# Attention tokens regrouped by batch, block 1's inputs held on chip, the inverse RMS passed through memory, constants merged, eight weight units decoded in the attention

## The chip, the cores and the metric

The kernel runs on one core of a Trainium2 chip. The metric is the time of one execution in device microseconds (us); the times of the kernel before are 832.14 us in the median of three runs, from 830.72 to 834.57. The engines are named TensorE (PE in the profile, its weight loads PEld), VectorE (DVE), ScalarE (ACT), GpSimd (POOL) and SyncE (SP). SyncE issues most of the DMAs; ScalarE and GpSimd issue some, each from its own queue of instructions.

## The reference

Four batches of 576 tokens go through a retention layer with 8 heads of 64, a gated MLP with RMS norm, and a mixture of 8 experts, one expert per token:

```python
scores = q @ k.T / sqrt(64)                   # per batch and head
ret = scores * where(rel >= 0, gamma[h] ** rel, 0)
x = (ret @ v).transpose(0, 2, 1, 3).reshape(2304, 512)

rms = sqrt(mean(x * x, -1) + 1e-6)
xn = x / rms * rms_g
g = xn @ w_gate                                # 512 -> 1536
x = (g / (1 + exp(-g)) * (xn @ w_val)) @ w_out # 1536 -> 512

logits = x @ w_gate2 + modality_bias[modality_id]
e = argmax(logits);  gate = softmax(logits)[e]
out = gate * (relu(x @ w1[e]) @ w2[e])         # 512 -> 1024 -> 512
```

The weights of the gated MLP are float32. Every product in the MLP and in the experts is made of three matmuls on high and low parts of both operands.

## The kernel before

The program is one order of instructions per engine, written out by hand; an engine takes its instructions in that order, and a semaphore makes it wait for operands of another engine.

*Attention.* The 576 tokens of a batch are five chunks: four of 128 and one of 64. The 20 steps g (batch b, chunk c) run through a loop over g from 0 to 20. One pass issues: the loads of step g + 7 (`a_load`, two DMAs into one of 8 buffers, SP), the decay of v for step g + 1 (`a_decay`, POOL, L297), the scores of step g (`a_scores`, PE L308, masks on DVE L312), the norm of step g - 3 (`a_norm1`), the running state (`a_state`, PE L327, copies on ACT L332 and L333), the product with V of step g - 1 (`a_pv`, PE L340 and L347, row scaling on DVE L352, square on ACT L354, sums on POOL L361 and L362), for g from 4 to 7 the norm of block 0 (`a_norm2`, DVE, a reciprocal L390 and a multiplication L391), a store of step g - 3 to the DRAM tensor `xnd` (`a_store`, from step 4 on), one tick of the weight pipeline (from pass 11 on) and for g from 7 to 10 the split of block 0's inputs into high and low parts (`split_x`, ACT L216 and DVE L217, four pairs of 128 columns). `a_norm1` sums squares over the partitions with a matmul against ones (L374) and takes the square root on ACT; from step 4 on the steps are summed in groups of up to 512 tokens, and a group's root goes to the DRAM tensor `rmsd` in one row.

*Weight units.* Each weight comes as 64-bit pieces that are rebuilt to 128x512 float32 on chip. A unit has three parts: `s0` the load (SP, 512 KB), `s1` the decode (ACT L135, DVE L136, L139, L142) and `s2` the split into high and low part (ACT L146, DVE L147). `pipe` issues per tick: `s1` of unit i, `s2` of unit i - 2, `s0` of unit i + lead. There are 24 units for the gate and value weights (two per feature tile f) and 12 for the output weights. Four of the first kind and one of the second go through the attention's passes (`prep_a`, lead 4, ticks from pass 11, the remaining ones behind the loop), the others through block 0 of the MLP (`prep_b`, lead 2; the last unit is cut in two halves).

*MLP.* The 2304 tokens are six blocks of 512, 512, 384, 384, 256 and 256. A block runs over 12 feature tiles f: `gv_mm` for gate and value (24 matmuls with as many columns as the block has tokens, PE L224 to L226), `gv_post` (SiLU on ACT L776, product on DVE L777, cast on ACT L778, difference on DVE L779), and the output product of tile f - 1 (`out_acc`, 3 matmuls of 512 columns per 128 tokens). In block 0 each f also carries 3 ticks of `prep_b`, f = 0, 4 and 8 carry 4. At f = 3 the inputs of the next block are loaded (`load_x`, and a row of `rmsd` sent to all partitions), from f = 5 on four pieces of `norm_x` (two reciprocals L199, two multiplications L202) prepare them, and behind f = 11 they are split. The routing of a finished block (per 128 tokens eight dot products L798, two groups of small operations on DVE, a matmul and an indirect store) is spread over the feature tiles of the next block as `bg`, `rate` pieces per f. The dot products write their unused full result into a part of the tile of the next block's inputs.

*Between attention and MLP.* The first gate product (`g0`), then `a_norm1` of the last two steps, then the first value product (`v0`).

*Experts.* Nine visits with fixed capacities read the tokens back by expert, with weights loaded and split on the way, and scatter the rows to the output by token number.

## Time and profile before

| | us |
|---|---|
| median of three runs | 832.14 |
| the runs, lowest and highest | 830.72, 834.57 |
| the profiled execution, whole time | 832.61 |
| its span from first to last instruction | 830.8 |

The page of the profile gives these busy times and slices:

```profile
PE 796.8 (96%) x4974; PEld 687.9 (83%) x4974; DVE 514.9 (62%) x1187; ACT 288.2 (35%) x555; POOL 98.2 (12%) x148
...
PE   8979889888999999999999999999999999999995
...
DVE  3878688887455636674563675747574555566650
...
PEclk9999999999999999999999999999999999999998
DMA  9997854337810000100100100051735264777400
```

Each of the 40 digits is a slice of 20.8 us, in tenths busy. The attention fills the first four and a half, block 0 the next five, the other blocks go on to slice 27 and the experts fill the rest. A timeline lists instructions by start and duration in us with engine, line and operation; the number in brackets is how long the engine was idle before and what released it. Matmul ends are modelled, so starts are the better measure there.

### The profile page before, as it was taken

How to read it: one execution, taken by the hardware profiler on the slowest of the kernel's cores; microseconds unless marked ns; L12 is line 12 of the kernel's file. 1: busy time of each engine (PE TensorE's matmuls, PEld its weight loads, DVE VectorE, ACT ScalarE, POOL GpSimd, SP SyncE). 2: the span in 40 equal slices, each digit the busy share in tenths (PEclk: the TensorE clock that was granted, in tenths of full speed). 3: DMA queues.
4: the chain of work that ended last, by engine and by line, in shares of the span. 5: the costliest groups of instructions: out<-in, count | busy, mean ns of one | idle time of the engine just before them, and what ended most of it. 6: DMA issues, size and time to landing. Idle time of an engine off the chain costs nothing.

```text
span 830.8 us, 13136 instructions
## 1 busy us (share of the span) xinstructions
PE 796.8 (96%) x4974; PEld 687.9 (83%) x4974; DVE 514.9 (62%) x1187; ACT 288.2 (35%) x555; POOL 98.2 (12%) x148
## 2 busy tenths in 40 slices
PE   8979889888999999999999999999999999999995
PEld 6868667656888889999999999999888898889894
DVE  3878688887455636674563675747574555566650
ACT  5445544434211131113111312134453444455530
POOL 4556100000000000100000001000100010010100
PEclk9999999999999999999999999999999999999998
DMA  9997854337810000100100100051735264777400
GB/s 313 323 360 225 267 202 152 98 117 270 287 61 14 13 14 25 51 14 14 33 13 14 45 15 27 14 189 68 253 123 174 77 217 145 277 249 235 142 19 13
DMA packets 48264, 107.21 MB, mean 129 GB/s; under 512 B 11266, under 2 KB 20998, under 8 KB 48072
## 3 DMA queue, kind: packets, MB, share of 16 engines
q1 hardware_dynamic: 43974, 96.37, 34.8%
q0 software_dynamic: 3168, 9.59, 3.0%
q8 instruction: 40, 0.66, 0.3%
q10 hardware_dynamic: 1058, 0.40, 0.2%
q14 instruction: 24, 0.20, 0.1%
HBM read 84.43 MB, written 22.83 MB: 129 GB/s over the span
## 4 chain that ended last, share of the span: by engine, by line
PE 76%; DVE 14%; issue 4%; ACT 2%; DMA 2%; POOL 1%; SPq 0%; another core or an unknown queue 0%; DVEq 0%; POOLq 0%; ACTq 0%
PE gv L224 10%; PE gv L225 10%; PE gv L226 10%; PE acc L224 10%; PE acc L226 10%; PE acc L225 10%; PE h L224 5%; PE h L225 4%; PE h L226 4%; DVE rawbt L139 2%; DVE rawbt L142 2%; DVE w L147 2%; DVE rawbt L136 1%; DVE pt L312 1%; PE tp L754 1%
## 5 line engine op out<-in xcount | busy, mean ns | idle before, releaser
L224 PE MATMUL gv<-xh,w 128*128 128x512 f32 (+2 forms) x576 | 196.5, 341 | 0.4 <-ACT scratch L776 0.4
L225 PE MATMUL gv<-xo,w 128*128 128x512 f32 (+2 forms) x576 | 194.1, 337 | 0.0
L226 PE MATMUL gv<-xh,w 128*128 128x512 f32 (+2 forms) x576 | 194.1, 337 | 0.0
L224 PEld LDWEIGHTS gv<-xh,w 128*128 128x128 f32 x576 | 109.2, 190 | 10.5 <-ACT scratch L776 0.9
L225 PEld LDWEIGHTS gv<-xo,w 128*128 128x128 f32 x576 | 109.2, 190 | 9.6 <-issue 0.4
L226 PEld LDWEIGHTS gv<-xh,w 128*128 128x128 f32 x576 | 109.1, 189 | 8.2 <-DVE w L147 0.3
L777 DVE TENSOR_TENSOR scratch<-gv,scratch 128x512 f32<-128x512 f32 (+2 forms) x72 | 39.9, 554 | 113.2 <-PE gv L226 113.1
L778 ACT CAST hh<-scratch 128x512 fp32r<-128x512 f32 (+2 forms) x72 | 37.0, 514 | 186.6 <-DVE scratch L777 186.6
L224 PE MATMUL acc<-wo,hh 128*128 128x512 f32 x216 | 86.9, 402 | 8.8 <-ACT hh L778 8.8
L707 DVE TENSOR_TENSOR w<-raw,w 128x1024 fp32r<-128x1024 f32 x64 | 78.1, 1225 | 27.0 <-ACT w L706 26.4
L798 DVE CUSTOM_DVE_ANT_0 xl<-row,wr 128x512 bf16<-128x512 f32 x128 | 87.8, 686 | 5.1 <-DMA xl<-xnd 2.5
L225 PE MATMUL acc<-wo,hh 128*128 128x512 f32 x216 | 86.3, 400 | 4.3 <-DVE wo L147 4.3
L224 PE MATMUL h<-xt,w 128*128 128x256 f32 (+3 forms) x288 | 88.9, 309 | 0.0
L226 PE MATMUL h<-xt,w 128*128 128x256 f32 (+3 forms) x288 | 87.4, 303 | 0.0
L225 PE MATMUL h<-xt,w 128*128 128x256 f32 (+3 forms) x288 | 87.3, 303 | 0.0
L226 PE MATMUL acc<-wo,hl 128*128 128x512 f32 x216 | 86.6, 401 | 0.0
L776 ACT ACTIVATE scratch<-gv 128x512 f32<-128x512 f32 (+2 forms) x72 | 35.3, 490 | 145.1 <-PE gv L226 131.6
L706 ACT CAST w<-raw 128x1024 fp32r<-128x1024 f32 x64 | 65.9, 1041 | 2.2 <-DMA raw<-in_w_dram 2.2
L779 DVE TENSOR_TENSOR hl<-scratch,hh 128x512 fp32r<-128x512 f32 (+2 forms) x72 | 40.2, 559 | 41.8 <-ACT hh L778 41.8
L224 PE MATMUL acc<-w,rh 128*128 128x512 f32 (+1 forms) x160 | 63.7, 398 | 0.0
L225 PE MATMUL acc<-w,rh 128*128 128x512 f32 (+1 forms) x160 | 63.3, 396 | 0.0
L226 PE MATMUL acc<-w,rl 128*128 128x512 f32 (+1 forms) x160 | 63.3, 395 | 0.0
(217 smaller groups left out, 1163.8 us busy)
## 6 DMA issues: line engine op xcount, KB each, us to landing
raw<-in_w_dram SPq DMA_DIRECT2D x64, 512.0 KB, 4.7
rawb<-in_wgv_dram SPq DMA_DIRECT2D x20, 512.0 KB, 3.5
xs<-zero SPq DMA_DIRECT2D x8, 1056.0 KB, 12.8
qk<-in_qkt_dram SPq DMA_DIRECT2D x16, 512.0 KB, 7.6
vk<-in_vkn_dram SPq DMA_DIRECT2D x16, 512.0 KB, 8.7
rawb<-in_wout_dram SPq DMA_DIRECT2D x10, 512.0 KB, 3.8
rowc<-xs SPq DMA_DIRECT2D x19, 264.0 KB, 4.4
xnd<-x SPq DMA_DIRECT2D x11, 256.0 KB, 6.2
```

The source lines that it names most:

```text
L139: DVE.scalar_tensor_tensor(out=u, in0=hw, scalar=-0x40000000, in1=u, op0=ALU.bitwise_and, op1=ALU.bitwise_or)
L142: DVE.tensor_tensor(out=u, in0=u, in1=lw, op=ALU.add)
L224: PE.matmul(ps, lh, rh, start=start, stop=False)
L225: PE.matmul(ps, lh, rl, start=False, stop=False)
L226: PE.matmul(ps, ll, rh, start=False, stop=stop)
L706: ACT.copy(out=w[:, 0, :], in_=raw)
L707: DVE.tensor_tensor(out=w[:, 1, :], in0=raw, in1=w[:, 0, :].bitcast(F32), op=ALU.subtract)
L776: ACT.activation(out=h, in_=gps[:, :n], func=ACTF.Silu)
L777: DVE.tensor_tensor(out=h, in0=vps[:, :n], in1=h, op=ALU.mult)
L778: ACT.copy(out=hh[:, :n], in_=h)
L779: DVE.tensor_tensor(out=hl[:, :n], in0=h, in1=hh[:, :n].bitcast(F32), op=ALU.subtract)
L798: DVE.tensor_tensor_reduce(out=junk, in0=row[:, 0:DM].rearrange("p (a b) -> p a b", a=2), in1=wr[:, e, :].rearrange("p (a b) -> p a b", a= ...
```

## The change

Six things, in the order of the file:

1. The blocks are 512, 512, 512, 256, 256, 256 tokens, and the tokens have another order: first the four whole chunks of batch 0, of batch 1, 2 and 3, then the four half chunks, two to a group of 128 (`home`). Three blocks are so the whole chunks of one batch. The token numbers in the rows, the modality and the bias follow that order.
2. Block 0's outputs of the attention stay in one tile `x0`, block 1's in the tile that takes the MLP's inputs (`x1`), and neither is stored; the others go to `xnd` in rows of 128 x 512, contiguous, half chunks in pairs.
3. `a_norm1` acts once per group (a batch's whole chunks, and the four half chunks) and puts the tokens on the partitions: one matmul with one column per 128 tokens, a root and a reciprocal of 128 x 4. The inverse goes to the DRAM tensor `rinv` from ACT's queue in the next pass (`a_inv`), and is read back by `load_inv` to all partitions, for block 0 in pass 9, also from ACT's queue. `norm_x` is then two multiplications of 128 x 1024 per 512 tokens, without reciprocal.
4. Block 0's norm and split are six pieces taken one per pass from pass 11 on (`bg0`): two multiplications and four splits, each of 512 columns.
5. Constants come in four DMAs instead of twelve: `early` (356 KB, ahead of the second step's loads), `keep` in pass 3, `brief` in pass 9, and `lcst` late. The second half of the loads of a 64-token step (k, which is not used there) is left out. The dot products of the routing write to a tile of their own, `sink`.
6. Eight gate and value units and one output unit go through the attention, with ticks from pass 4 on and 5 load buffers instead of 6; `prep_b` keeps 28 units.

The diff, cut to its core:

```diff
-BLOCKS = [512, 512, 384, 384, 256, 256]
+BLOCKS = [512, 512, 512, 256, 256, 256]
...
-XB = 7
+XB = 5
...
-NL2 = 4
-SX = 7
-NUA = 4
-PA, LD, RB = 11, 4, 6
+LX0, NX0 = 9, 11
+NUA = 8
+PA, LD, RB = 4, 4, 5
...
-    xnd = dram.tile([KD, 128, NT], F32, name="xnd")
-    rmsd = dram.tile([1, NT], F32, name="rmsd")
+    xnd = dram.tile([NC, 128, KD * 128], F32, name="xnd")
+    rinv = dram.tile([NT // 512 + 1, 512], F32, name="rinv")
...
+    def load_inv(j, rl, q=SP):
+        gr, o = divmod(STARTS[j], 512)
+        w = min(512, NT - gr * 512)
+        q.dma_start(out=rl[:, :w], in_=rinv[gr:gr + 1, :w].to_broadcast([128, w]))
+        return rl[:, :w].rearrange("p (t c) -> p c t", t=128)[:, o // 128:(o + BLOCKS[j]) // 128]
...
     def norm_x(j, xl, rl):
...
-        return [lambda: inverse(0), lambda: inverse(n // 2), lambda: scale(0), lambda: scale(2)]
+        def scale(c):
+            x, r = xl[:, c:c + 2], rl[:, c:c + 2]
+            DVE.tensor_tensor(out=x, in0=x, in1=r.unsqueeze(2).to_broadcast([128, 2, KD, 128]), op=ALU.mult)
+
+        return [lambda c=c: scale(c) for c in range(0, BLOCKS[j] // 128, 2)]
...
-    def split_x(x, parts, o, n):
+    def split_x(x, parts, n):
+        def piece(k):
+            hi, lo = (z[:, :n].rearrange("p (c t) -> p c t", t=128) for z in parts[k])
+            src = x[:, :n // 128, k, :]
+            ACT.activation(out=hi, in_=src, func=ACTF.Copy, scale=gt[:, k:k + 1])
...
+        return [lambda k=k: piece(k) for k in range(KD)]
...
+        groups = [[g for g in range(G) if steps[g][0] == b and steps[g][3] == 128] for b in range(B)]
+        groups.append([g for g in range(G) if steps[g][3] < 128])
...
+        def home(g):
+            b, c, o, n = steps[g]
+            return (b * NS0 + c, 0) if n == 128 else (B * NS0 + b * n // 128, b * n % 128)
...
+            w = DM if c + 1 == len(CHUNKS) else 2 * DM
+            SP.dma_start(out=vk.rearrange("p a d -> p (a d)")[:n, :w], in_=vkn[b, o:o + n, :w])
...
         def a_norm1(g):
...
+            for i in range(m):
+                PE.matmul(ss[:, i:i + 1], sq[:, i * 128:i * 128 + 128], ones, start=True, stop=True)
+            ri = att.tile([128, NS0], F32, tag="ri", name="ri", bufs=2)
+            ACT.activation(out=ri[:, :m], in_=ss[:, :m], func=ACTF.Sqrt, scale=1.0 / DM, bias=eps[:, 0:1])
+            DVE.reciprocal(out=ri[:, :m], in_=ri[:, :m])
+            i = home(gr[0])[0] // NS0
+            inv.append((rinv[i:i + 1, :n].rearrange("o (t c) -> (o t) c", c=m), ri[:, :m]))
+
+        def a_inv():
+            for dst, src in inv:
+                ACT.dma_start(out=dst, in_=src)
+            inv.clear()
...
             if g < G:
                 a_scores(g)
+            a_inv()
             if g >= 3:
                 a_norm1(g - 3)
+            if g == LX0:
+                bg0 += norm_x(0, x0, load_inv(0, rl0, ACT)) + split_x(x0, xsp, 512)
             if g < G:
                 a_state(g)
             if g >= 1:
                 a_pv(g - 1)
-            if NL2 <= g < NL2 + NS0:
-                a_norm2(g - NL2)
-            if g >= SD + NS0:
+            if g >= NX0 and bg0:
+                bg0.pop(0)()
+            if g >= SD:
                 a_store(g - SD)
...
-            if 0 <= g - SX < NS0:
-                split_x(x_t.pop(g - SX), xsp, 128 * (g - SX), 128)
...
         g0 = gv_mm(0, 0, xsp, BLOCKS[0])
         a_norm1(G - 2)
         a_norm1(G - 1)
+        a_inv()
         v0 = gv_mm(0, 1, xsp, BLOCKS[0])
...
-                    junk = x_in[0].bitcast(BF16)[:, 0:2, 768:1024]
+                    junk = sink.rearrange("p (a b) -> p a b", a=2)
...
-                    x_in[:] = [load_x(j + 1)]
-                    norm = norm_x(j + 1, x_in[0], row_tile(F32, "rl") if j else wr[:, 0, :])
+                    x_in[:] = [load_x(j + 1) if j else x1]
+                    rl = row_tile(F32, "rl") if j else wr[:, 0, :]
+                    norm = norm_x(j + 1, x_in[0], load_inv(j + 1, rl))
```

## Rows read from the trace of the kernel before

**Rows 1.** ScalarE's timeline at the first SiLU or ReLU of a block: start, duration, line, operation

```profile
212.52 0.60 ACT L776 ACTIVATE scratch<-gv 128x512 f32<-128x512 f32 x1 [2.11 <-PE gv L226]
...
311.73 0.49 ACT L776 ACTIVATE scratch<-gv 128x384 f32<-128x384 f32 x1 [1.47 <-PE gv L226]
...
462.77 0.38 ACT L776 ACTIVATE scratch<-gv 128x256 f32<-128x256 f32 x1 [0.80 <-PE gv L226]
...
566.93 0.38 ACT L899 ACTIVATE rh<-h 128x256 fp32r<-128x256 f32 x1 [1.49 <-PE h L226]
```

**Rows 2.** stage of block 4: us, busy PE, PEld, DVE, ACT, POOL; clock, DMA share, GB/s

```profile
461.00:512.00 51.00, 51.00 (x365) 47.30 (x364) 34.12 (x110) 11.40 (x29) 4.20 (x9) 1.00 0.09 30
```

**Rows 3.** VectorE's timeline in block 0: start, duration, line, operation, count

```profile
96.97 0.69 DVE L777 TENSOR_TENSOR scratch<-gv,scratch 128x512 f32<-128x512 f32 x1 [5.00 <-PE gv L226]
...
107.79 0.68 DVE L777 TENSOR_TENSOR scratch<-gv,scratch 128x512 f32<-128x512 f32 x1
...
117.25 0.68 DVE L777 TENSOR_TENSOR scratch<-gv,scratch 128x512 f32<-128x512 f32 x1
...
157.60 1.75 DVE L199 RECIPROCAL wr<-wr 128x256 f32<-128x256 f32 x1
...
179.74 1.22 DVE L202 TENSOR_TENSOR xl<-xl,wr 128x1024 f32<-128x1024 f32 x1
...
180.87 0.69 DVE L777 TENSOR_TENSOR scratch<-gv,scratch 128x512 f32<-128x512 f32 x1
```

**Rows 4.** TensorE's timeline, in brackets idle time before and what ended it

```profile
21.15 0.49 PE L374 MATMUL ss<-sq,ones 128*128 128x128 f32 x2
...
34.08 1.16 PE L308 MATMUL sc<-qk 64*128 64x128 f32 x16
...
91.46 1.73 PE L374 MATMUL ss<-sqs,ones 128*128 128x448 f32 x2 [2.29 <-POOL sqs L362]
...
195.35 0.50 PE L224 MATMUL acc<-wo,hh 128*128 128x512 f32 x1 [1.99 <-ACT hh L778]
```

**Rows 5.** busy us by stage, batches 1 to 3, and a stretch behind them

```profile
23.50:41.60 18.10, 17.65 (x264) 15.16 (x262) 17.28 (x25) 7.34 (x19) 10.60 (x13) 1.00 0.99 312
41.60:65.20 23.60, 18.97 (x262) 15.32 (x261) 16.14 (x30) 11.06 (x28) 12.38 (x19) 1.00 1.08 343
65.20:86.10 20.90, 19.29 (x284) 16.35 (x282) 19.21 (x36) 9.71 (x20) 12.55 (x15) 1.00 0.75 234
...
91.40:95.00 3.60, 3.54 (x7) 2.34 (x8) 0.57 (x1) 1.23 (x2) 0.01 (x1) 0.53 0.73 208
```

**Rows 6.** VectorE's timeline in loops 7 and 8 of the attention

```profile
35.09 0.93 DVE L390 RECIPROCAL ri<-ri 128x128 f32<-128x128 f32 x1
36.06 1.20 DVE L391 TENSOR_TENSOR x<-x,ri 128x512 f32<-128x512 f32 x1
...
39.23 1.27 DVE L312 TENSOR_TENSOR pt<-sc,causal 128x512 f32<-128x512 f32 x2
...
42.47 2.47 DVE L217 SCALAR_TENSOR_TENSOR xo<-x,gt,xh 128x128 fp32r<-128x128 f32 x4 [1.38 <-ACT xh L216]
```

**Rows 7.** VectorE's timeline in loop 17 of the attention

```profile
74.99 1.27 DVE L312 TENSOR_TENSOR pt<-sc,causal 128x512 f32<-128x512 f32 x2
...
76.79 0.41 DVE L136 TENSOR_SCALAR rawt<-raw 128x512 int32<-128x512 int32 x1
...
78.22 0.85 DVE L142 CUSTOM_DVE_ANT_0 rawt<-raw,rawt 128x1024 uint16<-128x1024 uint16 x1 [0.30 <-ACT raw L135]
78.99 0.94 DVE L147 TENSOR_TENSOR w<-rawt,w 128x512 fp32r<-128x512 f32 x1
79.86 1.28 DVE L312 TENSOR_TENSOR pt<-sc,causal 128x512 f32<-128x512 f32 x2
```

**Rows 8.** DMA issues, the rms gains' load: count, KB, us to landing

```profile
gt<-in_rmsg_dram SPq DMA_DIRECT2D x1, 2.0 KB, 8.5
```

**Rows 9.** one line's operations, L147: min/median/max ns, first and last start

```profile
L147 DVE TENSOR_TENSOR w<-rawbt,w x20: 683/684/687, 104.7 to 197.2; 128x512 fp32r<-128x512 f32 x20
```

More of the change, by code (lines that the diff above doesn't have):

```diff
@@ L265 @@
         G = len(steps)
-        qk_t, vk_t, pt_t, x_t, sq_t, ri_t = {}, {}, {}, {}, {}, {}
-        groups, sums = [], {}
-        for g in range(NS0, G):
-            n = steps[g][3]
-            if not groups or sum(steps[i][3] for i in groups[-1]) + n > 512:
-                groups.append([])
-            groups[-1].append(g)
-        place = {g: (gr, sum(steps[i][3] for i in gr[:z])) for gr in groups for z, g in enumerate(gr)}
+        qk_t, vk_t, pt_t, x_t, sums, bg0, inv = {}, {}, {}, {}, {}, [], []
+        groups = [[g for g in range(G) if steps[g][0] == b and steps[g][3] == 128] for b in range(B)]
+        groups.append([g for g in range(G) if steps[g][3] < 128])
+        place = {g: (gr, sum(steps[i][3] for i in gr[:z])) for gr in groups for z, g in enumerate(gr)}
+        x0 = att.tile([128, NS0, KD, 128], F32, name="x0")
+        rl0 = att.tile([128, 512], F32, name="rl0")
+        x1 = x_tile()
+        def home(g):
+            b, c, o, n = steps[g]
+            return (b * NS0 + c, 0) if n == 128 else (B * NS0 + b * n // 128, b * n % 128)
         def by_pair(ps):
@@ L350, in a_pv @@
                     )
-            x = att.tile([128, NP, 128], F32, tag="x", name="x", bufs=XB)
-            DVE.tensor_tensor(out=x[:, :, :n], in0=pv[:, :, :n], in1=rc[:, :, o:o + n], op=ALU.mult)
-            sq = att.tile([128, NP, 128], F32, tag="sq", name="sq", bufs=4)
-            ACT.activation(out=sq[:, :, :n], in_=x[:, :, :n], func=ACTF.Square)
-            total = sq[:, 0, :n]
-            if g >= NS0:
-                gr, o = place[g]
-                if not o:
+            hc, ho = home(g)
@@ new lines, in a_pv @@
+            if hc < 2 * NS0:
+                x = (x0 if hc < NS0 else x1)[:, hc % NS0]
+            else:
+                if not ho:
+                    x_t[hc] = att.tile([128, NP, 128], F32, tag="x", name="x", bufs=XB)
+                x = x_t[hc][:, :, ho:ho + n]
+            DVE.tensor_tensor(out=x, in0=pv[:, :, :n], in1=rc[:, c, :, :n], op=ALU.mult)
+            sq = att.tile([128, NP, 128], F32, tag="sq", name="sq", bufs=4)
+            ACT.activation(out=sq[:, :, :n], in_=x, func=ACTF.Square)
@@ L359, in a_pv @@
+            gr, o = place[g]
+            if not o:
+                if n == 128:
                     sums[gr[0]] = att.tile([128, 512], F32, tag="sqs", name="sqs", bufs=2)
-                total = sums[gr[0]][:, o:o + n]
+                else:
+                    sums[gr[0]] = att.tile([128, 256], F32, name="sqh")
             POOL.tensor_tensor(out=sq[:, 0:2, :n], in0=sq[:, 0:2, :n], in1=sq[:, 2:4, :n], op=ALU.add)
-            POOL.tensor_tensor(out=total, in0=sq[:, 0, :n], in1=sq[:, 1, :n], op=ALU.add)
@@ L363, in a_pv @@
-            x_t[g], sq_t[g] = x, sq
+            POOL.tensor_tensor(out=sums[gr[0]][:, o:o + n], in0=sq[:, 0, :n], in1=sq[:, 1, :n], op=ALU.add)
         def a_norm1(g):
-            n, sq = steps[g][3], sq_t.pop(g)[:, 0, :]
-            if g >= NS0:
-                gr, o = place[g]
-                if g != gr[-1]:
-                    return
-                n, sq = o + n, sums.pop(gr[0])
-            ss = ps_g("ss")
-            PE.matmul(ss[:, :n], ones, sq[:, :n], start=True, stop=True)
-            if g < NS0:
-                ri = att.tile([128, 128], F32, tag="ri", name="ri", bufs=3)
-            else:
-                ri = att.tile([128, 512], F32, tag="rig", name="rig", bufs=2)
@@ L379, in a_norm1 @@
[L379 to L393 removed]
+            gr, o = place[g]
@@ new lines, in a_norm1 @@
+            if g != gr[-1]:
+                return
+            n, sq = o + steps[g][3], sums.pop(gr[0])
+            m = n // 128
+            ss = ps_g("ss")
+            for i in range(m):
[3 more added lines that the diff above has]
+            DVE.reciprocal(out=ri[:, :m], in_=ri[:, :m])
@@ L423 @@
             a_load(g)
-        SP.dma_start(out=ident, in_=cst[:, 0:128])
         POOL.memset(ones16, 1.0)
@@ L465 @@
                 POOL.memset(cum, 0.0)
-            if g == 11:
-                SP.dma_start(out=m64, in_=mod.bitcast(I32).rearrange("p (c two) -> p c two", two=2))
-                SP.dma_start(out=b8, in_=bias)
+            if g == 9:
+                SP.dma_start(out=temp, in_=brief)
             if g == 14:
@@ L767 @@
         wr = bp.tile([128, E, DM], F32, name="wr")
+        sink = bp.tile([128, DM], BF16, name="sink")
         def scratch():
```

152 lines of the change are left out of this document (61 added, 91 removed).

## Prediction

> **What bounds the kernel now.** I read the busy time by stage first, then the timelines of VectorE, TensorE and ScalarE at the seams between stages. Call loop g the g-th of the 20 attention steps, unit one 128x512 weight tile to be rebuilt from its 64-bit form, tick one call of the pipeline that does it, and f the 12 feature tiles of a block of the first MLP.
>
> From block 1 to the end of block 5 TensorE has no idle time: between the first SiLU of block 1 and the first ReLU of the expert stage lie 354.4 us [rows 1], and in block 4 it is busy 51.00 of 51.00 us [rows 2]. VectorE's savings there are worth nothing. The losses sit earlier. In block 0 the MULT of VectorE (L777) comes every 9.46 us (107.79 to 117.25) [rows 3] where block 1 shows that TensorE can do a feature tile in 8.27 us (99.2 us for twelve from 212.52 to 311.73) [rows 1]: VectorE has 1.98 us of its own there (two products and the wait for the cast between them) and three ticks of 2.49 us (9.46 - 1.98 over 3). Feature tiles 0, 4 and 8 carry four ticks, two carry a reciprocal of 1.66 us and two a scaling of 1.13 us [rows 3]. TensorE's last idle time in it ends at 195.35, behind L777 of f = 9 [rows 3, 4]. In the attention both engines are nearly full in batch 1 (TensorE 17.65, VectorE 17.28 of 18.10 us), batch 2 takes 23.60 us for the same work of TensorE and batch 3 20.90 us [rows 5]. So block 0 pays 98.38 us from its first L777 (96.97) to that last stall, and what the change moves is VectorE's work, from block 0 into the attention.
>
> **Attention, loops 0 to 8.** Removed: in loops 4 to 7 a reciprocal (0.97 us start to start) and a scaling (about 1.15 us), in loops 7 to 10 four split products (2.1 to 2.5 us, with up to 1.38 us of waiting for ScalarE ahead) [rows 6]. Without them VectorE has nothing but the masks and the row scaling, 1.8 us per loop, until ticks compute. The masks of loop 8 started at 39.23 although the scores were there from 34.08 + 1.1 = 35.2 [rows 4, 6]. They follow the scores now, so 35.2, and three sums over partitions of some 0.4 us each (0.49 as recorded [rows 4]) leave TensorE's path ahead of that while one group's eight short ones enter (0.3 us, an estimate by their count): 34.3 us, 4.9 us earlier. The merged constant load of 356 KB stands where 28, 64 and 256 KB stood; what the first decay waits for is longer, but the first scores stand behind the warm-up and the second decay behind its own load. Costed at nothing, from -0.5 to +0.5 us.
>
> **Attention, loops 8 to 16.** Nine units instead of five now decode inside the loop, the decode at loops 8 to 16, the split at 10 to 18. A full loop with both cost 4.87 us (74.99 to 79.86), 0.87 of it the last product and 0.3 a wait for ScalarE [rows 7]. Loop 8 has no split: 4.0. Loop 9, with 64 tokens in place of 128: 3.5. Loop 10: 4.6. Loops 11 and 12 add block 0's scaling of 128x1024, 1.13 us as in [rows 3]: 6.0 each. Loops 13 to 16 add one split of 128x512 each: the wait for ScalarE's square and cast (about 1.2 us, as the 1.38 us ahead of the product at 42.47 [rows 6]) and the product (0.65 us, an estimate by the 0.6 to 0.7 us of every 128x512 product here), less the 0.3 us wait that then lies within: 6.4, loop 14 with half the masks and the bias arithmetic 6.9, loop 15 5.9, loop 16 6.4. Sum 49.7 us. Then loops 17 to 19 and the last product with V: before 11.1 us (74.99 to 86.10), now without the two decodes of 2.2 us in it [rows 5, 7]: 6.7. The attention ends at 34.3 + 49.7 + 6.7 = 90.7, 4.6 us later than 86.10.
>
> **Its tail.** From 86.10, the end of batch 3 [rows 5], to the first L777 [rows 3] lie 10.87 us. [...] With no tick left in loop 19 the sums come while the first gate product runs. 10.87 - 3.9 = 7.0, so the first L777 stands at 97.7, 0.7 later than before. The two stores of the inverse and their wait for VectorE's reciprocal stand ahead of the SiLU on ScalarE; one such store and its issue stood there before. Bounds for this 5.5 to 9 us.
>
> **Block 0.** To L777 of f = 8 VectorE took 83.9 us (96.97 to 180.87) [rows 3]. The ticks per feature tile are the same in number; gone are two reciprocals (3.3), and both of block 1's scalings instead of one now come before that point (+1.1): 81.7. There the two kernels part: of 28 units only two half ones and the last splits are left, some 6.3 us with VectorE's own 1.98, so f = 8 no longer binds and TensorE runs at 8.27 from then on. Its resumption at f = 9, 98.38 us after the first L777 before, comes at 81.7 + 1.4 + 8.3 = 91.4: 7.0 us gained. Weights are two tiles further ahead, so the small waits for output weights go too; they are inside the 9.46.
>
> **The rest.** 512, 384, 384, 256, 256 columns become 512, 512, 256, 256, 256. By the seams of [rows 1] a 512 block takes 99.2 us, a 384 block 75.5 (462.77 - 311.73, halved), a 256 one 52.1 (566.93 - 462.77, halved): 151.3 against 151.0 us, +0.3. Block 3 (256) now routes the four chunks of a 512 block; block 4 before routed three with VectorE busy 34.12 of 51 us [rows 2], and one chunk more is eight dot products and two groups of small operations, an estimate of 34.12/3 less the products of the block itself, some 8 us: 42 of 52. It fits; 0 to 2 us if its lag outgrows the PSUM buffers. Reciprocals, the separate sink of the dot products and contiguous loads are off the path. The same tokens go to the same experts, so the expert stage is unchanged.
>
> **DMA.** The weights of eight units (4.2 MB) now go ahead of the last attention load, about 1.8 MB of stores and half vk loads go away. The queue is full until batch 2 ends (share 0.99 to 1.08) but 0.75 in batch 3 [rows 5], so it was ahead of the engines by then, and the attention takes 4.6 us longer. I take nothing; up to 5 us if the queue falls behind in loops 10 to 13. The inverse is written as 128 pieces of 16 bytes at loop 7 and read at loop 9, two loops (about 8 us) later. Nearest is the load of 16-byte pieces, 8.5 us to landing in the full queue [rows 8]: ScalarE, which issues the read, could wait 0 to 2 us, with the copies of the state queued behind it and TensorE's products behind those; I take 0, since ScalarE has no full loop there.
>
> **The sum.** +0.7 - 7.0 + 0.3 = -6.0 us on the profiled execution (832.61, of which its span is 830.8 and 1.8 lie around it, taken as unchanged): 826.6. The median, 832.14, is 0.5 lower: 826.
>
> **Rivals.**
> 1. *VectorE and POOL collide more.* The last product of a unit takes 0.94 us at 78.99 in the attention, where POOL works beside it, and 0.684 (median) in block 0, where POOL is idle [rows 7, 9]. My loops hold that as measured. If the other two-input products are lengthened by the same 0.26 us, it is 18 more of the nine units, four splits and two scalings: 24 x 0.26 = 6, so 832. For it: the scaling of 128x512 at 36.06 took 1.20 us, the one of 128x1024 in block 0 1.22 [rows 3, 6]. Against: in the loops at 74.99 the same POOL work runs and the sum fits. [...]
> 2. *Loads fall behind.* As above, +5: 831. Decides when a load lands after its decay could start.
> [...]
> 4. *The attention is no longer than before.* If the waits for ScalarE vanish in the longer loops and the catch-up at the end is better than 6.7, the 4.6 us do not arise: 821.
> 5. *The change does not move the work.* If block 0 stays bound elsewhere, the 7.0 go: 833.
>
> **How the numbers follow.** Forecast 0.50 (own range 822 to 830), rival 1 0.13, 2 0.10, 3 0.09, 4 0.14, 5 0.04. The likeliest gives 826. From 820 to 834 leaves out half of rival 4 and rival 3. About 0.5% is what a measurement of this kernel can tell from no change: under 828.0 is faster, over 836.3 slower. Over four fifths of the forecast and all of rival 4 are faster: 0.57. Most of rival 3 is slower: 0.08. The rest 0.35.
>
> **What would show it.** Masks of loop 8 near 34; loops 11 to 16 near 6 us with VectorE without idle time; the last product with V near 91; no idle time of TensorE ahead of the sums; first L777 near 98; feature tile 8 at 8.3 us; block 0 about 7 us shorter from the first L777; blocks 1 to 5 again 354 us. Clock under 1 in the attention, a decay that waits for vk, or idle TensorE in block 3 would make it wrong, and so would an attention of other length than 91 us.

## The result, and the profile after

The changed kernel takes 842.16 us (median of 4 runs, 841.26 to 843.00) against 832.71 us (4 runs, 830.72 to 834.57) for the kernel before, both measured side by side: a ratio of 1.0114, 95% interval 1.0085 to 1.0142. It is 1.1% slower; the forecast was 826, with a range of 820 to 834. The profiled execution has a span of 841.2 us, 10.4 more than before, and a mean granted clock of 0.974 (before 0.993).

Where the time came from is read at the seams first. ScalarE's and VectorE's timelines of the kernel after, at the first MULT of block 0 (L782, the L777 of before), the first SiLU of block 1 and the first ReLU of the experts:

```profile
112.77 0.69 DVE L782 TENSOR_TENSOR scratch<-gv,scratch 128x512 f32<-128x512 f32 x1 [2.57 <-PE gv L229]
...
223.59 0.60 ACT L781 ACTIVATE scratch<-gv 128x512 f32<-128x512 f32 x1 [2.16 <-PE gv L229]
...
577.78 0.38 ACT L906 ACTIVATE rh<-h 128x256 fp32r<-128x256 f32 x1 [1.49 <-PE h L229]
```

Against [rows 1] the first SiLU of block 1 is 11.1 us late (223.59 against 212.52), the first ReLU 10.9 us (577.78 against 566.93). So blocks 1 to 5 take 354.2 us as before, and everything was lost ahead of block 1. The first MULT of block 0 came at 112.77 against 96.97 [rows 3], 15.8 us late; from there to block 1 the change won 4.7. The attention lost it. Three stretches of it (us, busy PE, PEld, DVE, ACT, POOL, then clock, DMA share, GB/s):

```profile
39.90:67.60 27.70, 20.20 (x268) 17.14 (x266) 24.86 (x34) 10.11 (x22) 14.85 (x15) 0.92 1.04 358
67.60:86.00 18.40, 15.86 (x136) 13.93 (x136) 14.77 (x25) 7.58 (x16) 7.68 (x10) 0.50 0.16 63
86.00:104.00 18.00, 14.39 (x159) 11.81 (x158) 13.72 (x23) 6.14 (x13) 6.76 (x8) 0.87 0.23 78
```

VectorE is busy 24.86 of 27.70 us in the first, which holds loops 9 to 12 and most of their ticks, TensorE only 20.20; and TensorE's clock, 1.00 in batches 1 to 3 before [rows 5], stands at 0.92, 0.50 and 0.87. Two causes offer themselves, and both are in these rows: a VectorE with no time left, and a TensorE at half its clock. VectorE's timeline at the masks of loop 8, its row scaling, and the masks of loops 14, 15 and 17:

```profile
34.53 1.29 DVE L322 TENSOR_TENSOR pt<-sc,soon 128x512 f32<-128x512 f32 x2 [0.39 <-PE sc L318]
37.28 0.69 DVE L368 TENSOR_TENSOR xl<-pv,soon 128x512 f32<-128x512 f32 x1 [1.45 <-PE pv L357]
...
72.43 0.74 DVE L322 TENSOR_TENSOR pt<-sc,soon 64x256 f32<-64x256 f32 x2
...
80.37 1.28 DVE L322 TENSOR_TENSOR pt<-sc,soon 128x512 f32<-128x512 f32 x2
...
94.69 1.28 DVE L322 TENSOR_TENSOR pt<-sc,soon 128x512 f32<-128x512 f32 x2
```

VectorE's timeline of loop 12, from its masks to those of loop 13, with GpSimd's of the same time:

```profile
57.31 1.27 DVE L322 TENSOR_TENSOR pt<-sc,soon 128x512 f32<-128x512 f32 x2
58.51 0.67 DVE L368 TENSOR_TENSOR x<-pv,soon 128x512 f32<-128x512 f32 x1
59.10 2.06 DVE L205 TENSOR_TENSOR x<-x,rl 128x1024 f32<-128x1024 f32 x1
61.08 0.42 DVE L132 TENSOR_SCALAR rawt<-raw 128x512 int32<-128x512 int32 x1
61.54 1.10 DVE L135 SCALAR_TENSOR_TENSOR rawt<-raw,rawt 128x512 int32<-128x512 int32 x1
62.78 0.72 DVE L138 CUSTOM_DVE_ANT_0 rawt<-raw,rawt 128x1024 uint16<-128x1024 uint16 x1
63.42 1.53 DVE L143 TENSOR_TENSOR w<-rawt,w 128x512 fp32r<-128x512 f32 x1
64.87 1.27 DVE L322 TENSOR_TENSOR pt<-sc,soon 128x512 f32<-128x512 f32 x2
...
60.01 2.09 POOL L377 TENSOR_TENSOR sq<-sq 128x256 f32<-128x256 f32 x1 [3.17 <-ACT sq L370]
62.17 0.78 POOL L378 TENSOR_TENSOR sqs<-sq 128x128 f32<-128x128 f32 x1
62.91 1.48 POOL L307 TENSOR_TENSOR vk<-vk,soon 64x512 f32<-64x512 f32 x1
```

There is no idle time in these 7.56 us, where the forecast had 6.0. The scaling (L205) takes 2.06 us where [rows 3] has 1.22; the second decode step (L135) takes 1.10 and the last product of a unit (L143) 1.53, where a product of this size takes 0.68 with GpSimd idle [rows 9]. The last two began while a GpSimd operation ran (L377 and L307); the scaling began ahead of one (59.10 against 60.01). GpSimd's operations too are long: the decay (L307) takes 1.48 here, and 1.04 in an earlier loop, where VectorE has next to no work:

```profile
27.96 1.04 POOL L307 TENSOR_TENSOR vk<-vk,soon 128x512 f32<-128x512 f32 x1
```

The groups of VectorE's operations of loops 10 to 19 (count, busy us, mean ns, idle time before them), and what it waited for in the same stretch (total, times, longest):

```profile
L135 DVE SCALAR_TENSOR_TENSOR rawt<-raw,rawt 128x512 int32<-128x512 int32 x7 | 8.5, 1220 | 0.2
L143 DVE TENSOR_TENSOR w<-rawt,w 128x512 fp32r<-128x512 f32 x8 | 7.3, 912 | 1.3 <-ACT w L142 1.3
L132 DVE TENSOR_SCALAR rawt<-raw 128x512 int32<-128x512 int32 x7 | 4.8, 683 | 1.2 <-DMA raw<-in_wgv_dram 1.2
L205 DVE TENSOR_TENSOR x<-x,rl 128x1024 f32<-128x1024 f32 x2 | 4.1, 2054 | 0.0
...
DVE xo L219 <- ACT xh L218: 5.3, 4, 1.4
DVE w L143 <- ACT w L142: 1.3, 1, 1.3
DVE wo L143 <- ACT wo L142: 1.3, 1, 1.3
```

### The profile page after: what moved, and what is told of

Same layout as the page of the kernel before. It is cut to its first block, busy times and chain, and to the rows that moved or that the text cites. A ratio compares the mean times of both kernels' runs of the same rounds, so it can differ in the third digit from the quotient of the medians.

```text
span 841.2 us, 13114 instructions
## 1 busy us (share of the span) xinstructions
PE 808.1 (96%) x4994; PEld 689.5 (82%) x4994; DVE 505.7 (60%) x1161; ACT 283.3 (34%) x540; POOL 105.0 (12%) x148
## 4 chain that ended last, share of the span: by engine, by line
PE 77%; DVE 12%; DMA 4%; issue 4%; ACT 2%; POOL 1%; SPq 0%; another core or an unknown queue 0%; DVEq 0%; POOLq 0%; ACTq 0%
PE gv L227 10%; PE gv L229 10%; PE gv L228 10%; PE acc L227 10%; PE acc L229 10%; PE acc L228 10%; PE h L227 4%; PE h L228 4%; PE h L229 4%; DVE rawbt L135 2%; DMA vk<-in_vkn_dram 2%; DVE w L143 2%; DVE rawbt L138 1%; DMA raw<-in_wgv_dram 1%; PE tp L758 1%
## 5 line engine op out<-in xcount | busy, mean ns | idle before, releaser
L227 PE MATMUL gv<-xh,w 128*128 128x512 f32 (+1 forms) x576 | 196.1, 340 | 0.2 <-ACT scratch L781 0.2
L229 PE MATMUL gv<-xh,w 128*128 128x512 f32 (+1 forms) x576 | 194.5, 338 | 0.0
L228 PE MATMUL gv<-xo,w 128*128 128x512 f32 (+1 forms) x576 | 194.4, 338 | 0.0
L782 DVE TENSOR_TENSOR scratch<-gv,scratch 128x512 f32<-128x512 f32 (+1 forms) x72 | 40.0, 556 | 124.9 <-PE gv L229 124.8
L783 ACT CAST hh<-scratch 128x512 fp32r<-128x512 f32 (+1 forms) x72 | 37.0, 514 | 192.5 <-DVE scratch L782 192.5
L803 DVE CUSTOM_DVE_ANT_0 sink<-row,wr 128x512 bf16<-128x512 f32 x128 | 88.2, 689 | 2.6
L781 ACT ACTIVATE scratch<-gv 128x512 f32<-128x512 f32 (+1 forms) x72 | 35.3, 491 | 138.6 <-PE gv L229 132.7
L784 DVE TENSOR_TENSOR hl<-scratch,hh 128x512 fp32r<-128x512 f32 (+1 forms) x72 | 40.2, 559 | 41.8 <-ACT hh L783 41.8
```

The lines of the kernel that those rows point to most:

```text
L227: PE.matmul(ps, lh, rh, start=start, stop=False)
L228: PE.matmul(ps, lh, rl, start=False, stop=False)
L229: PE.matmul(ps, ll, rh, start=False, stop=stop)
L781: ACT.activation(out=h, in_=gps[:, :n], func=ACTF.Silu)
L782: DVE.tensor_tensor(out=h, in0=vps[:, :n], in1=h, op=ALU.mult)
L783: ACT.copy(out=hh[:, :n], in_=h)
```

## Theories and experiments

*Theory A*: VectorE's chain in loops 10 to 16 sets the length; the four more units, the dear scaling, the waits and the stretched operations stand in it. *Theory B* (rival 3, a clock that falls in the attention): TensorE's halved clock sets the length. *Theory C*: on GpSimd the decay of the next chunk is queued behind the square sums, which wait for a late VectorE; the state products wait for the decay. Every run below is compared with the kernel before on the same chip, where that took 832.3 to 832.7 us. "End" is the start of the last row scaling on VectorE, "f = 0" the first MULT of block 0, "block 1" its first SiLU; all in us, from the profiled run.

| kernel | time | ratio, 95% interval | end | f = 0 | block 1 |
|---|---|---|---|---|---|
| before | 832.71 | | 89.06 | 96.97 | 212.52 |
| after | 842.16 | 1.0114 (1.0085-1.0142) | 103.97 | 112.77 | 223.59 |
| a_nua4 | 830.65 | 0.9975 (0.9964-0.9986) | 90.78 | 98.03 | 211.98 |
| b_nua8b | 836.65 | 1.0063 (1.0046-1.0080) | 96.97 | 105.19 | 215.89 |
| a_fill | 844.30 | 1.0150 (1.0133-1.0167) | 106.85 | 114.00 | 224.49 |
| a_dec | 842.91 | 1.0131 (1.0114-1.0148) | 103.35 | 111.92 | 222.75 |
| a_ct | 845.18 | 1.0165 (1.0143-1.0187) | 107.73 | 114.99 | 223.96 |
| a_swap | 836.87 | 1.0063 (1.0046-1.0080) | 99.68 | 106.84 | 217.29 |
| a_swcp | 833.83 | 1.0023 (1.0011-1.0035) | 97.62 | 104.83 | 213.80 |
| a_pesum | 854.12 | 1.0257 (1.0224-1.0290) | 115.54 | 123.78 | 233.86 |
| a_best1 | 824.38 | 0.9913 (0.9896-0.9929) | 86.57 | 92.53 | 204.91 |
| a_best2 | 842.08 | 1.0126 (1.0109-1.0143) | 102.47 | 110.26 | 222.56 |
| a_best3 | 825.10 | 0.9927 (0.9910-0.9943) | 87.36 | 92.67 | 205.57 |
| a_best4 | 828.79 | 0.9969 (0.9954-0.9984) | 92.55 | 97.85 | 208.94 |

**Which part of the change it is: a_nua4 and b_nua8b.** One undoes the units alone (their number, first pass and load buffers), the other makes them alone. b_nua8, the second without its last edit, needs 147.25 KB per partition for the attention's tiles where 145.625 KB are left, and has no time.

```diff
 # a_nua4, on the kernel after
-NUA = 8
-PA, LD, RB = 4, 4, 5
+NUA = 4
+PA, LD, RB = 11, 4, 6
 # b_nua8b, on the kernel before; the second "rig" tile goes to make room
-NUA = 4
-PA, LD, RB = 11, 4, 6
+NUA = 8
+PA, LD, RB = 4, 4, 5
-    ri = att.tile([128, 512], F32, tag="rig", name="rig", bufs=2)
+    ri = att.tile([128, 512], F32, tag="rig", name="rig", bufs=1)
```

> The changed kernel with the weight units of the attention put back to four, from loop 11 on, with six raw buffers; all other parts of the change stay. Theory A (VectorE's work in loops 10 to 16, made by the four extra units) expects the last product of the attention at 87 to 91 us instead of 103.9, the first gv product of block 0 (f = 0) at 95 to 98 instead of 112.8, block 0 longer again by some 4 to 6 us, and a span of 828 to 832. Theory B (the halved TensorE clock) expects the same end only if the clock of loops 11 to 19 is back at 0.95 or more. A rival, that not the units but the six pieces of block 0's norm and split in loops 11 to 16 make the loss, expects the attention to end after 96 and a span of 836 or more.

> The kernel before with one part of the change alone: eight weight units in the attention from loop 4 on and five raw buffers; to find room for them one of the two tiles for the root of a group's mean goes. Theory A (the four extra units lengthen VectorE's chain in the attention by more than block 0 gives back) expects the last product of the attention 7 to 14 us later than 86.1, block 0 some 3 us shorter, and a time of 836 to 844 us. The rival, that the units cost this much only beside the six pieces of block 0 that the change puts into loops 11 to 16, expects the attention to end before 91 and a time of 828 to 834.

With four units the end is back at 90.78 and f = 0 at 98.03, as theory A had it. This alone does not part theory A from theory B, as the clock is back too (1.00 from 39.9 to 67.6 us, 0.91 from there to 86). The four units cost 13.2 us of attention (103.97 - 90.78) and give back 3.1 in block 0, less than the 4 to 6 expected: from f = 0 to block 1 it takes 110.8 us with eight (223.59 - 112.77), 113.95 with four (211.98 - 98.03). The rest of the change together is worth -0.25% (830.65 against 832.47 on that chip): a small gain. On the kernel before, the same units cost 8.2 us up to f = 0 and give back 4.9: 836.65, within the bounds, though at their low end. Up to 1.2 of the 8.2 us may be the missing tile's and not the units', since ScalarE's first SiLU waits there for the store of the root to land, which it does not in the kernel before (1.23 us before it starts at 104.56). So the units lose by themselves, by some 3 to 4 us, and by 11.5 us in the surroundings that the other parts of the change make. One difference shows in VectorE's groups from loop 8 on (count, busy us, mean ns) of b_nua8b:

```profile
L139 DVE SCALAR_TENSOR_TENSOR rawt<-raw,rawt 128x512 int32<-128x512 int32 x9 | 6.2, 693 | 0.3
L136 DVE TENSOR_SCALAR rawt<-raw 128x512 int32<-128x512 int32 x9 | 3.7, 412 | 0.0
```

The same nine units (eight and one output weight), and their first two decode steps take 0.69 and 0.41 us, not 1.22 and 0.68 as L135 and L132 after the change.

**Is it the clock? a_fill.**

```diff
+        def filler(g, ps):
+            if g >= 10:
+                for _ in range(6):
+                    PE.matmul(ps, ones16, wide, start=True, stop=True)   # wide: 128 x 512, BF16
         # a_scores(g), ahead of its products
+            filler(g, scs[0].rearrange("p a t -> p (a t)"))
         # a_pv(g - 1), ahead of its products
+            filler(g + 1, pv.rearrange("p a t -> p (a t)"))
```

> The changed kernel with filler products on TensorE in loops 10 to 19: six of 128 x 512 in BF16 ahead of the scores and six ahead of the value products, into the same PSUM tiles, whose results are overwritten. VectorE's work is untouched. Theory B (the clock sets the length) expects a granted clock of 0.95 or more between 67 and 104 us, score and value bursts near 1.1 us instead of 2.1, the attention's end at 98 or before (103.9 without filler) and a span of 835 or less. Theory A (VectorE's chain sets the length, the clock is only its consequence) expects the clock to rise as well, the attention's end within 1.5 us of 103.9, and a gain of 1 to 2 us at most, from the first gv product, which ran at a clock of 0.57: a span of 839 to 842.

The stretches of the kernel with the filler (columns as above), and the masks of loops 14 and 15:

```profile
39.90:67.60 27.70, 27.19 (x292) 18.55 (x297) 23.76 (x34) 9.45 (x20) 14.59 (x14) 1.00 1.00 348
67.60:86.00 18.40, 17.43 (x175) 11.73 (x177) 14.07 (x26) 7.76 (x16) 7.36 (x10) 1.00 0.26 95
86.00:104.00 18.00, 17.02 (x180) 11.93 (x180) 13.73 (x22) 6.67 (x14) 6.78 (x9) 1.00 0.15 48
...
73.94 0.74 DVE L329 TENSOR_TENSOR pt<-sc,soon 64x256 f32<-64x256 f32 x2
...
81.88 1.28 DVE L329 TENSOR_TENSOR pt<-sc,soon 128x512 f32<-128x512 f32 x2
```

The clock is at 1.00 in all three, and loop 14 takes 7.94 us (73.94 to 81.88), the same as after the change at a clock of 0.50 (72.43 to 80.37); so does loop 15 with 6.86 us in both (81.88 to 88.74, and 80.37 to 87.23). Theory B falls for the loops: with TensorE's waits filled the clock stays up, and the low clock had cost nothing there. What it did cost is behind them: from the end to f = 0 the changed kernel takes 8.80 us, this one 7.15, so 1.65 us is the price of the low clock in the first gate product (0.57 from 104 to 108 us after the change). The end itself comes 2.9 us later than after the change, where theory A allowed 1.5: loop 10 takes 7.62 us instead of 6.13, and VectorE waits 1.54 us for the last product with V. Hence 844.3.

**Is it GpSimd's queue? a_dec.**

```diff
-            if g + 1 < G:
-                a_decay(g + 1)
+            if g == 0:
+                a_decay(1)
+            if g + 2 < G:
+                a_decay(g + 2)
```

> The changed kernel with the GpSimd decay of a chunk issued one loop earlier (two chunks ahead), so that it no longer stands behind the square sums of the loop before. Theory C (the decay queued behind the sums delays the state products, and with them the clock) expects the state product's waits of 3.67 and 2.10 us for GpSimd to be gone, the clock between 56.9 and 67.6 us above 0.95 instead of 0.82, the attention's end 3 to 6 us earlier and a span of 835 to 838. Theory A expects the end within 1 us of 103.9 and a span of 840 to 842, because VectorE had next to no idle time in loops 10 to 16.

What TensorE waited for in loops 10 to 19 (total us, times, longest), first of the kernel after, then of this one:

```profile
PE st L337 <- POOL vk L307: 6.6, 3, 3.7
PE pv L357 <- DVE pt L322: 5.4, 5, 2.9
```

```profile
PE pv L357 <- DVE pt L322: 10.5, 12, 2.6
PE st L337 <- POOL sqs L378: 1.7, 1, 1.7
```

The waits for the decay, 6.6 us, are gone, and the waits for VectorE's masks grew from 5.4 to 10.5. The end moves by 0.6 us. Theory C falls: the queue on GpSimd was where TensorE happened to wait, not what held the loop.

**What the scaling costs: a_ct.** The inverse is stored by chunk, then token, so that VectorE reads neighbours.

```diff
-            inv.append((rinv[i:i + 1, :n].rearrange("o (t c) -> (o t) c", c=m), ri[:, :m]))
+            inv.append((rinv[i:i + 1, :n].rearrange("o (c t) -> (o t) c", c=m), ri[:, :m]))
-        return rl[:, :w].rearrange("p (t c) -> p c t", t=128)[...]
+        return rl[:, :w].rearrange("p (c t) -> p c t", t=128)[...]
```

> The changed kernel with the inverse rms stored in the order chunk, token, so that the scaling reads it with a step of one element instead of four; its stores then write single elements of 4 bytes. If the step is what makes the scaling of two chunks slow (2.05 us in the attention, 1.97 in block 0), it falls to 1.1 to 1.3 us in both, the attention ends 1.0 to 1.7 us earlier and block 0 is 1 to 1.6 us shorter: a span of 837.5 to 839.5. If it is the shape of the operands (four dimensions, inverse broadcast over the middle one), or the activity of GpSimd, the duration stays at 1.9 to 2.1 us and the time stays within 1 us.

The line of the scaling (min, median and max ns, first and last start), of block 1's two scalings, which run in block 0 with GpSimd idle; first the kernel after, then this one:

```profile
L205 DVE TENSOR_TENSOR xl<-xl,wr x2: 1964/1964/1965, 173.7 to 185.0; 128x1024 f32<-128x1024 f32 x2
```

```profile
L205 DVE TENSOR_TENSOR xl<-xl,wr x2: 1218/1218/1218, 175.9 to 186.5; 128x1024 f32<-128x1024 f32 x2
```

The step of four elements (16 bytes) is what costs: 1.96 us against 1.22 us for the same 128x1024. The kernel after shows a step of two as well: block 5 consists of the half chunks, whose group is 2 x 128 tokens in place of 4 x 128, so that its scaling reads the inverse with a step of two elements (8 bytes), and there it takes no longer than with a step of one:

```profile
496.64 1.22 DVE L205 TENSOR_TENSOR xl<-xl,rl 128x1024 f32<-128x1024 f32 x1
```

Block 0 gets 1.9 us shorter (108.97 against 110.82 from f = 0 to block 1), a little more than expected. Yet the kernel is slower, where 837.5 to 839.5 had been expected of the span: in loop 9 VectorE waits 5.13 us for a unit's weights, and between 39.9 and 67.6 us the DMA moves 259 GB/s in place of 358. I put that down to the single-element stores, the only transfers that the edit changes, but no run isolates it; a step of one is bought at the wrong place here. For 1024 elements the trace shows 0.75 us more at a step of four (1.96 against 1.22) and nothing more at a step of two.

**The waits and the copy: a_swap and a_swcp.**

```diff
-            if g >= NX0 and bg0:
-                bg0.pop(0)()
             if g >= SD:
                 a_store(g - SD)
             if g >= PA:
                 next(prep_a, lambda: None)()
+            if g >= NX0 and bg0:
+                bg0.pop(0)()
 # a_swcp, besides
+            if g == NX0:
+                ACT.copy(out=fl0, in_=rv0)      # the loaded inverse, in order; the same for block 1 at f = 5
```

> The changed kernel with the two lines of a loop exchanged: the weight tick is issued ahead of the piece of block 0's norm or split. The four splits of loops 13 to 16 each made VectorE wait some 1.37 us for ScalarE's rounded copy; behind the tick the copy is ready before VectorE comes to it. If VectorE's chain is the bound, these 5.3 us of waits are worth 4 to 5.5 us: the attention's end at 98.5 to 100 and a time of 836.5 to 838.5. If something else holds loops 13 to 16 (TensorE at half clock, the state products behind GpSimd), another wait takes their place and the end moves by less than 2 us.

> The changed kernel, with its eight units, and both edits of the fastest run: tick ahead of the piece, inverse copied by ScalarE. It shows whether the price of the four extra units (11.5 us between 842.2 and 830.7) depends on what stands beside them. If the prices add up, the copied inverse takes another 3 us off the run with the exchanged lines (836.9): 833 to 835, and the four extra units still cost 8.5 to 10.5 us against 824.4. If the time that the scaling frees only lets GpSimd's sums meet VectorE's decode instead, the time stays at 836 or more and the attention's end within 1 us of 99.7.

The exchanged lines are worth 5.3 us (842.16 - 836.87), the copy another 3.0 (to 833.83), both as theory A had it. The four extra units still cost 9.5 us (833.83 against 824.38, the same edits with four): the prices nearly add up, the two edits being worth 8.3 us with eight units and 6.3 with four. How the time comes is more telling than its sum. VectorE's groups of loops 10 to 19 with the lines exchanged:

```profile
L135 DVE SCALAR_TENSOR_TENSOR rawt<-raw,rawt 128x512 int32<-128x512 int32 x7 | 4.8, 693 | 0.2
L219 DVE SCALAR_TENSOR_TENSOR xo<-x,kept,xh 128x512 fp32r<-128x512 f32 x4 | 6.1, 1525 | 0.0
L205 DVE TENSOR_TENSOR x<-x,rl 128x1024 f32<-128x1024 f32 x2 | 5.6, 2820 | 0.0
```

The 5.3 us of waits for ScalarE are gone, and L135 is back from 1.22 to 0.69. But the split (L219) went from 0.77 to 1.53 and the scaling from 2.05 to 2.82: the operation that now begins while GpSimd's decay runs is the one that is stretched. It shows most plainly with the copied inverse, whose scaling takes 1.22 us when GpSimd is idle. A scaling of VectorE and the decay of GpSimd beside it, in a_swcp:

```profile
54.22 2.06 DVE L205 TENSOR_TENSOR x<-x,fl 128x1024 f32<-128x1024 f32 x1
...
53.71 1.49 POOL L308 TENSOR_TENSOR vk<-vk,soon 128x512 f32<-128x512 f32 x1
```

VectorE's operation starts at 54.22, GpSimd's ends at 55.20 (53.71 + 1.49); from there 1.22 us of work would end at 56.42, and it ended at 56.28. So it waited for nearly all that was left of the other. In the loop 12 shown above, L143 starts at 63.42, the decay ends at 64.39, and 0.69 us behind that is 65.08: it ended at 64.95.

**GpSimd's sums on TensorE: a_pesum and a_best2.**

```diff
-                PE.matmul(ss[:, i:i + 1], sq[:, i * 128:i * 128 + 128], ones, start=True, stop=True)
+                    for k in range(NP):
+                        PE.matmul(ss[:, i:i + 1], sq[i][:, k, :], ones, start=k == 0, stop=k + 1 == NP)
 # whole chunks: no POOL.tensor_tensor; the norm one loop earlier; six square tiles in place of four
```

> The changed kernel with the square sums of the whole chunks taken from GpSimd: TensorE adds them, with four products of one column per chunk in place of one, and the norm of a batch comes one loop earlier. Theory A1 (VectorE's decode is stretched by the GpSimd sums and decays that now run beside it) expects the decode's operations in loops 10 to 16 back at 0.42 and 0.69 us (they averaged 0.68, 1.22 and 0.91 for its first, second and last step), the attention's end 4 to 7 us earlier and a time of 836 to 839. Theory A2 (it is the number of VectorE's operations; the stretch is hidden elsewhere, or the decay alone gives the same stretch) expects the end within 2 us of 103.9 and a time of 840 to 844.

> The changed kernel with four weight units from loop 11 on, the tick ahead of block 0's pieces, the inverse rms of block 0 and block 1 copied once on chip by ScalarE so that the scaling reads it with a step of one, and the square sums of whole chunks on TensorE. From the run with four units (830.7 us, attention's end at 90.8): the exchanged lines are worth up to 5 us, the scalings 1.7 us in the attention and 1.5 us in block 0, the sums up to 3 us where VectorE bounds loops 11 to 16. Theory A expects the attention's end at 82 to 85 (TensorE's own work in the loops is the next bound) and a time of 821 to 825. If another wait takes over, the end stays at 87 or later and the time at 827 or more.

The first is slower than either theory had it, the second came out where another wait takes over (842.08), and not for the reason under test. VectorE's operations did get shorter (the means of L135 from 1.22 to 0.85 and of L143 from 0.91 to 0.70), though L135 not back to the 0.69 of theory A1. But TensorE's 32 products of one column took 3.73 us where a_nua4, at full clock too, takes 1.05 for its eight, and then this happened (TensorE's timeline of a_pesum and its stretches, columns as above):

```profile
23.63 3.73 PE L394 MATMUL ss<-ones,sq 128*128 128x1 f32 x32
...
26.00:30.00 4.00, 4.00 (x39) 3.75 (x38) 0.18 (x1) 1.00 (x3) 0.00 (x0) 0.71 1.11 292
30.00:34.00 4.00, 4.00 (x51) 3.66 (x52) 1.29 (x3) 0.42 (x1) 1.82 (x4) 0.50 0.99 364
```

The clock went to 0.50 while the engine is recorded busy without a gap; in the kernel after, busy 4.00 of 4.00 us in both of these stretches too, it stays at 1.00. So this edit answers the question on VectorE's operations, but not what taking the sums from GpSimd would be worth; that stays open.

**A version that beats both: a_best1, a_best3, a_best4.** Four units, tick first, copied inverse, sums left on GpSimd; the second with the units from loop 4 on and the pieces in loops 14 to 19; the third as the second with six units.

```diff
 # a_best1, besides a_swcp's edits
+NUA = 4
+PA, LD, RB = 11, 4, 6
 # a_best3: PA, LD, RB = 4, 4, 6 and LX0, NX0 = 12, 14; a_best4: the same with NUA = 6, RB = 5
```

> The run with four weight units (830.7 us, attention's end at 90.8) with two more edits: the tick ahead of block 0's pieces, and the inverse rms of block 0 and block 1 copied once by ScalarE so that the scaling reads it with a step of one; the square sums stay on GpSimd. Theory A expects 2 to 4 us from the exchanged lines (four waits of 1.16 to 1.39 us go, some of it comes back as stretched operations, as in the run with the lines alone), 1 to 1.7 us from the scalings in the attention and 1.5 us from those of block 0: a time of 824 to 826.5. If the stretch eats it all, 828 to 830.

> As the run before in this list (four units, inverse copied, tick first), but with the units from loop 4 on and block 0's six pieces in loops 14 to 19, so that no loop has both a full tick and a piece. If what counts is VectorE's work in a single loop against TensorE's 4.0 us of products, the ticks make loops 8 to 14 some 0.5 us longer each and the pieces hide: the attention ends at 86 to 88, the first gv product of block 0 comes at 93 to 95, and the time is 821 to 825. If VectorE's total counts, wherever it stands, the time is that of the run before in this list within 1 us.

> As the run before in this list, but with six units in place of four. The two more units cost VectorE some 5 us in loops 12 to 16, of which TensorE's products hide 2 to 3, and give back 1.5 us in block 0: 0.5 to 2 us slower than with four units. If units were free wherever no piece stands beside them, it would be 1 to 2 us faster than with four.

a_best1 takes 824.38 us, 0.87% less than the kernel before (0.71 to 1.04%) and 2.1% less than the changed one (824.38 / 842.16). The first of the three stretches in it:

```profile
39.90:67.60 27.70, 26.21 (x396) 22.85 (x392) 19.65 (x35) 12.22 (x26) 16.95 (x24) 1.00 1.01 350
```

TensorE is busy 26.21 of 27.70 us in it, against 20.20 after the change: it is nearly full there, and VectorE (19.65) has time to spare. Moving the pieces apart from the ticks (a_best3) is no better than putting the tick first, 825.10 against 824.38, which is what was expected if VectorE's total counts; its clock is at 0.79 from 67.6 to 86 us, with TensorE recorded busy all through; what it loses there I did not follow further. Six units are 3.7 us slower than four, more than the 0.5 to 2 expected.

## Why the prediction was wrong

Outside loops 8 to 19 most steps stood. The masks of loop 8 came at 34.53 (34.3 forecast, though its 0.3 us for the eight short sums was an estimate without a row, and they took 1.05 at 27.05 on L389), from f = 8 on block 0 runs ahead of VectorE (f = 9 follows f = 8 by 6.66 us, 196.39 to 203.05, before by 13.1), blocks 1 to 5 take 354.2 us and block 3 with its four chunks cost nothing; loads fell behind once, by 1.2 us. The prediction summed to 824.8 on the span; it was 841.2, and the 16.4 us divide so:

- **Loops 8 to 16: forecast 49.7, measured 60.2 (34.53 to 94.69): +10.5.** This is the step that failed. By the groups above and the durations that b_nua8b has for the same steps, L135 took 0.53 us too much, seven times (3.7); L132 0.27, seven times (1.9); the two scalings 0.83 more than 1.22 each (1.7); one wait for a load 1.2: 8.5 of 10.5. Another 1.45 stands in loop 8 (the row scaling at 37.28 above): VectorE waits there for TensorE's product with V, and the 4.0 us of the forecast held VectorE's own work alone. The rest are smaller terms of both signs. So the term with the largest error is the decode of a unit, priced at what it takes beside other neighbours; its first two steps alone are 5.6 us.
- **Within that, the scaling was priced by the wrong row.** Its 1.13, from start to start, came from [rows 3] (1.22 as a duration), where the inverse lies in order; the change reads it with a step of four. Alone that makes 1.96 (a_ct). The diff shows the step, and I read it and went past it.
- **Within that, the stretch beside GpSimd was counted at a fraction.** Rival 1 had this mechanism and gave it 0.26 us a time, from the 0.94 of [rows 7], and 0.13 as its chance. That its total of 6 us is near the 5.6 of the two decode steps is luck: it spread 24 small losses where mainly 14 larger ones fell. It took the 0.94 for the price of every meeting. In the runs VectorE's operation waited for nearly all that was left of GpSimd's: 0.84 us more for a product of 0.69 (L143, 1.53 at 63.42), 0.84 more for a scaling of 1.22 (2.06 at 54.22 in a_swcp). The 0.94 of before was a meeting with a shorter operation, GpSimd's sum of 128x128 (0.46 us at 22.18 after the change, with VectorE idle):

  ```profile
  78.60 0.79 POOL L362 TENSOR_TENSOR sqs<-sq 128x128 f32<-128x128 f32 x1
  ```

  The sum ends at 79.39, and 0.69 us behind that is 80.08: the product of [rows 7] ended at 79.93 (78.99 + 0.94). The decay, which is longer, came next, at 79.34 beside the masks at 79.86 [rows 7], and those took no longer for it. So "the sum fits" in rival 1 held for that order of the loop only; the scalings and splits, put ahead of the tick, and in loop 10 the late load, brought the decode beside the decay. How much is lost is decided by where in the loop the two meet; my rows showed two such meetings, 0.94 and, at 36.06 [rows 6], 1.20 for a product that takes 0.69 at 28.81 in the same trace, and I took the smaller as the price.
- **Loops 17 to 19 and the last product: 6.7 forecast, 9.2 measured (94.69 to 103.9): +2.5.** I took the decodes out of these loops and left the splits in, without the wait that the splits then have: with no decode between, VectorE waits 1.3 us for ScalarE's cast in L143, twice. The removed work had been the cover of that wait.
- **The tail: 7.0 forecast, 8.8 measured.** The 3.9 us taken off were the 2.29 of idle time [rows 4] and some 1.6 for the low clock behind it (0.53 [rows 5]), and no run shows the second term. After the change the sums came in time, as forecast, and TensorE is busy 8.80 of 8.80 us; but the low clock did not go away (0.57 from 104 to 108 us), and costs 1.65 (a_fill).
- **Block 0: -7.0 forecast, -4.7 measured** (110.82 against 115.55 from f = 0 to block 1). Two scalings at 1.96 instead of 1.22 are 1.5 of the 2.3, and a_ct, which takes that away, gains 1.9 there.

These four differences make 17.1 us; the masks of loop 8 add 0.2, and from block 1's first SiLU to the end the kernel took 1.0 less than forecast (617.6 against 618.6).

Rival 3, a slower kernel by a clock that falls in the attention, had the right sign, and the clock does fall (0.50 between 67.6 and 86), but it was wrong as a cause: with the clock held at 1.00 loops 11 to 16 were as long, within 0.1 us each. The chance of 0.08 for a slower kernel was too small because the forecast and rival 1 were added up from bare durations: VectorE had some 6 us of work in loops whose TensorE needs 3.9 (17.65 us in batch 1 [rows 5], for four whole chunks and a half one), so every further us on VectorE counted in full, while of the four units' work only 3.1 us came back in block 0.

## What to carry to other kernels

Work that is moved from one stage to another is priced where it lands: at full length where its engine is already the bound there, with every wait that the work taken out had covered and every operation of another engine that it now meets. Here a duration from another row held only for the same access step and the same neighbours. When a clock falls together with a longer stage, hold the clock up with filler (1.00 in all three stretches of a_fill) before believing that it is the cause.

## What the runs showed of the hardware

- These operations of VectorE, begun while one of GpSimd was at work, ended as if they had begun when that one ended, to within 0.15 us: L135 and L143, wherever they met one in loops 10 to 16 after the change (L135 from 53.98, beside a sum that ends at 54.53: 0.69 us behind that is 55.22, and it ended at 55.08), and the scaling in a_swcp. The first decode step (L132), with one input, did so too: in loop 15 it takes 1.26 us from 83.90, beside a decay that ends at 84.87, and 0.42 alone. The row scaling (L368), one of whose operands is in PSUM, did not wait: 0.69 us at 22.67 beside a decay from 22.60 to 23.64. The decay took 1.49 us from 55.35, where L138 of VectorE had begun ahead of it and ended at 55.93 (1.04 behind that is 56.97, and it ended at 56.84), against 1.04 at 27.96.
- Reading one operand with a step of 16 bytes made a 128x1024 product 1.96 us instead of 1.22; a step of 8 bytes did not (1.22). This loss and the wait add up: in a_swap a scaling begins at 62.03, the decay ends at 63.00, 1.96 us behind that is 64.96, and it ended at 64.83. Where the scaling began ahead of GpSimd's operation it took 2.06 (59.10 after the change).
- TensorE's granted clock fell to 0.50 (30 to 34 us) behind 32 products of one column in a_pesum, although the engine is recorded busy 4.00 of 4.00 us; in a_best2, which has the same sums, it is 0.80 from 22.5 to 39.9 us, as in a_pesum. The busy share in a profile, where the ends of matmuls are modelled, did not tell that the clock would hold: it is the same 4.00 of 4.00 us in the kernel after, at 1.00.
